# Scaling the first two tiles' queries in halves, a bank clear and a low part moved to VectorE, and a new queue order in a gated-recurrence plus two-MLP kernel

## The chip, the core and the metric

The kernel runs as one program on one core of a Trainium2 chip. The metric is device time in microseconds (us) of one execution; several executions are timed and the median is taken. Beside these, one further execution was profiled; its trace gives every row that is shown below.

## What is computed

The reference runs a gated linear recurrence over 768 steps for 4 batches of 8 heads (48 channels each), and sends its output through two MLPs. All values are 32-bit floats.

```python
for t in range(S):
    state = alpha[:, :, t, :, None] * state + k_t (outer) v_t
    y[:, :, t] = q_t . state
x = y as 3072 tokens of 384 channels
h = x @ w_in;  x = (h * cos(h)) @ w_out              # MLP 1, 2048 wide
h = max(x @ w1, x @ w2, x @ w3);  out = h @ w_out    # MLP 2, 768 wide
```

## The kernel before

**Units.** The tokens are cut into six units of 512. The recurrence of a unit is computed in tiles of heads: cumulative products of alpha (scans on VectorE, DVE in the rows) give factors with which keys and queries are scaled (GpSimd, POOL), TensorE (PE) makes scores of scaled keys with scaled queries, VectorE masks them, and PE multiplies the masked scores with the values. The first unit has its own code: three tiles of 128 rows, `chain0` (scans and scalings), `scores0` and `shared_scores0` (scores of the tile's own heads, and of the heads that are spread over the tiles), `values0` and `shared_values0` (products with the values, which add up in three PSUM banks `acc[0..2]`), `outputs0` (the sums go to SBUF as a high part, copied by ScalarE (ACT), and a low part), `transposes0` and `state0` (the state that the next unit starts from). Later units use `turn` (transposes) and `visit` (scores and states of one tile; then, as a second part, the products of a tile visited before).

**MLP 1.** It is written in steps `moe1(i)`, 96 of them, 16 per unit. A step has nine hidden matmuls (lines 763 to 765, three per group of channels `cc`; they read the unit's `xt` of that group, high and low part, and a weight's high and low part), a chain on the result, and nine output matmuls (lines 794 to 796). The chain alternates between two engines: ACT copies to whole turns (771), DVE subtracts them (772), ACT takes the sine (773), DVE multiplies (775 or 783), ACT rounds to the high part `gh` (776 or 784), DVE subtracts for the low part `gl` (777 or 789). Lines 794 and 795 of the output need `gh` alone, line 796 needs `gl`.

**Weights.** The blocks of MLP 1's weights come in by DMA while the first unit runs, and each is unpacked and split by ACT (387, 392), DVE (388, 394) and POOL (396). The weights of MLP 2 are prepared the same way later (`b_prep`, `out_prep`), and MLP 2 follows when all units are through MLP 1.

**Order.** Every operation is recorded with an engine, a planned duration, what it reads and writes, and a due time. `Program.order` plays the program through with these figures and so fixes one order per engine; each engine then works its queue strictly in that order. Constants in the head of the file (`LATE`, `ATT0`, `V2`, `MOE_EARLY`, `SLOW` and others) set due times and planned durations, so a constant can move work on all five queues. PSUM banks `ps0` to `ps4` are handed out in the same pass. Where the plan sees PE idle in the first 45 us, a filler matmul is put in (the last lines of `tile_kernel`); the kernel before has none.

Of the kernel before, what the change touches and what calls it, by code (L numbers as in the profile page):

```python
# [16 lines left out]
AF = mybir.ActivationFunctionType  # L17
# [9 lines left out]
P = 128  # L27
# [33 lines left out]
B_START, B_STEP = 17.76, 2.27  # L61
# [8 lines left out]
GLE1, GLQ = 0, 15  # L70
# [3 lines left out]
XLE = (0,)  # L74
# [4 lines left out]
GATE, GSTEP = 0, 3  # L79
LGATE = 11  # L80
W0 = -0.9
LATE, LATE_S = -3.58, -4.98
LOD = (1, 3)

W1E = 21
MOE_EARLY = 5
EARLY = 3
FIRST = -4
ATT0 = 3.97
ATTS = 3.25  # L90
VIS, VEND, VQ = 3.95, 12, 0.98
LARGE, STALL, PATIENT = 2, -0.53, 2.75
V2, V2S, TA = 16.24, 2.98, 0.97
# [168 lines left out]
def pool(n):  # L262
    return 0.16 + 0.0021 * n
# [16 lines left out]
SLOW = 1.2  # L280
# [3 lines left out]
def dma(nbytes):  # L284
    return max(nbytes, 15e3)
# [11 lines left out]
def tile_kernel(ctx, tc, aa, qk, vv, vr, wt, outT):  # L297
# [147 lines left out]
    def load0():  # L445
        def alpha(k):
            return ("inf", k), lambda: nc.sync.dma_start(al_f[k], aa[0, k, :, 0:KO]), P * KO * 4

        def keys(k, h):
            return ("inq" if h else "ink", k), lambda: nc.sync.dma_start(kq_f[k][:, HB * h:HB * (h + 1)], qk[0, k, :, HB * h:HB * (h + 1)]), P * HB * 4  # L450

        def vals(k):
            return ("v", k), lambda: nc.sync.dma_start(v_b[k], vv[0, k]), P * HB * 3

        def shared_vals():
            return "vr", lambda: nc.sync.dma_start(rest, vr.rearrange("p (i j k e) -> p i j k e", i=N2, j=2, e=32)), P * N2 * 2 * NT0 * 128

        for n, (key, f, b) in enumerate((alpha(0), keys(0, 0), alpha(1), keys(0, 1), keys(1, 0), alpha(2), keys(1, 1), keys(2, 0), keys(2, 1), vals(0), vals(1), vals(2), shared_vals())):
            op("SP", HW, f, (), [key], -40 + 0.1 * n, 0.95 * dma(b) if n else 0)

    def chain0(k):
        t, gf, kg = al_f[k], g_f[k % NGS], ("g", k % NGS)
        g = gf[:, 0:AP].rearrange("p (c t) -> p c t", c=N2)
        fv = t[:, 0:AP].rearrange("p (c t) -> p c t", c=N2)
        kv3, qv3 = views0(k)
        kf, kk, kq, ka = ("inf", k), ("ink", k), ("inq", k), ("acc", 2)
        t0 = -30 + k
        ones, seeds = acc[2][:, 0:AP // 2], acc[2][:, HB - AP // 2:][:, ::-1]
        for h in range(2):
            hs = slice(AP // 2 * h, AP // 2 * (h + 1))  # L470
            op("DVE", 0.07 + 0.00208 * AP / 2, lambda hs=hs: ve.tensor_tensor_scan(
                gf[:, 0:AP][:, ::-1][:, hs], t[:, 1:AP + 1][:, ::-1][:, hs], ones, 0.0, ALU.mult, ALU.add), [ka, kf, *([("scan", k - 1)] if k else [])], [(*kg, h)], t0)
        op("Pool", pool(HB), lambda: ge.tensor_tensor(kv3, kv3, g[:, :, 1:], ALU.mult), [(*kg, 0), (*kg, 1)], [kk], t0)
        op("Act", act(HB), lambda: se.activation(kr_b[k], kq_f[k][:, 0:HB], AF.Copy, scale=shared), [kk, "shared"], [krk[k]], t0)
        for h in range(2):
            hs, cs = slice(AP // 2 * h, AP // 2 * (h + 1)), slice(N2 // 2 * h, N2 // 2 * (h + 1))
            op("DVE", 0.15, lambda cs=cs: ve.reciprocal(seeds[:, ::CP], g[:, cs, 0]), [ka, (*kg, 1 - h)], ["seeds"], t0)
            op("DVE", 0.07 + 0.00208 * AP / 2, lambda hs=hs: ve.tensor_tensor_scan(
                t[:, hs], t[:, hs], seeds, 0.0, ALU.mult, ALU.add), [ka, "seeds", (*kg, 0), (*kg, 1)], [kf, ("scan", k)], t0)
        op("Pool", pool(HB), lambda: ge.tensor_tensor(qv3, qv3, fv[:, :, 1:], ALU.mult), [kf], [kq], t0)  # L480

    def scores0(k, n, t):
        rk, r = psum2("r0")
        kv3, qv3 = views0(k)

        def amm():
            for i in range(N2):
# [3 lines left out]
        op("PE", SLOW * 0.95, amm, [("ink", k), ("inq", k)], rk, t, tiled=True, count=32)  # L491
        return mask0(n, r, rk, t + 0.01)

    def shared_scores0(n, t):
        rk, r = psum2("r0")

        def amm(k):
            kr3, qv3 = kr_b[k].rearrange("p (c t) -> p c t", c=N2), views0(k)[1]
            for i in range(N2):
# [4 lines left out]
        for k in range(NT0):  # L504
            op("PE", SLOW * 0.95, lambda k=k: amm(k), [krk[k], ("inq", k)], rk, SR + k if k < 2 else t, tiled=True, count=32)
        return mask0(n, r, rk, t + 0.01)

    def clear0(k):
        m = zero.rearrange("p (a b) -> p a b", a=1).to_broadcast([P, 4, P])
        op("PE", 0.25, lambda: pe.matmul(acc[k].rearrange("p (a b) -> p a b", a=4), zero, m, start=True, stop=False, skip_group_check=True),  # L510
           ["zero"], [("acc", k), *(["seeds"] if k == 2 else [])], -27)
# [29 lines left out]
    def transposes0(k, t):  # L541
# [7 lines left out]
        op("PE", SLOW * N2 * 0.085, trans, [("ink", k), "ident", ("y1", LGATE)], [pk_k], t, count=2 * N2)  # L549
# [24 lines left out]
    def first_unit():  # L574
# [31 lines left out]
    def prepare(n, t0):  # L606
# [8 lines left out]
        op("SP", HW, lambda: nc.sync.dma_start(al_f[na], aa[u, p, :, 0:KO]), (), [kf], t0 - 4.8 + (0.8 if not k else 0), dma(PR * KO * 4), tiled=True)  # L615
        op("SP", HW, lambda: nc.sync.dma_start(kq_f[nk], qk[u, p]), (), [kk, kq], t0 - 3.9, dma(PR * 2 * HB * 4), tiled=True)
# [819 lines left out]
```

## Time and profile before

| what | value |
|---|---|
| median of the timed executions | 739.07 us (3 runs, 739.06 to 739.8) |
| the profiled execution, its own time | 738.83 us |
| its span, first to last instruction | 736.9 us |
| PE busy | 730.0 us, 99% of the span |
| DVE, ACT, POOL busy | 539.7 us (73%), 420.1 us (57%), 303.8 us (41%) |
| granted clock of PE | 1.00 in all 40 slices |

Times in rows count from the start of the span. What lies outside the span, 1.9 us of the profiled execution's time, belongs to start and end of the launch. A matmul's duration in a row is modelled and overlaps the next one's; what a matmul costs is read from start to start.

### The profile page before, as it was taken

The numbers are of one execution on the slowest core, as the hardware profiler recorded it, in microseconds if no ns is written. First come the engines' busy times: TensorE is split into PE (matmuls) and PEld (weight loads), VectorE is DVE, ScalarE is ACT, GpSimd is POOL, SyncE is SP. The second block draws the span as 40 slices with busy tenths as digits, with TensorE's granted clock in tenths as the row PEclk, the third lists the DMA queues.
The fourth block names the chain that finished last, engine by engine and source line by source line (L and its number), as shares of the span: only waits on it lengthen the run. The fifth ranks groups of instructions, "written<-read, shape, count | busy, mean of one in ns | idle before, by whom it ended". The sixth has DMA issues, their size and how long they took to land.

```text
span 736.9 us, 14861 instructions
## 1 busy us (share of the span) xinstructions
PE 730.0 (99%) x5815; PEld 600.8 (82%) x5815; DVE 539.7 (73%) x858; ACT 420.1 (57%) x801; POOL 303.8 (41%) x284
## 2 busy tenths in 40 slices
PE   8999999999999999999999999999999999999997
PEld 6788888888888888888888888888888888888886
DVE  7999996877877776865655666467787768677763
ACT  4888866666756666667644655443563345634233
POOL 6444433556533635454320211043465543614442
PEclk9999999999999999999999999999999999999999
DMA  8866534564644554554250111397625556246302
GB/s 319 298 226 212 171 126 134 176 222 158 206 139 154 187 181 136 184 180 148 98 207 0 44 43 44 140 368 292 213 103 201 198 177 205 77 149 206 130 1 85
DMA packets 47525, 120.41 MB, mean 163 GB/s; under 512 B 4736, under 2 KB 19968, under 8 KB 42464
## 3 DMA queue, kind: packets, MB, share of 16 engines
q1 hardware_dynamic: 47456, 119.48, 47.4%
q8 instruction: 45, 0.74, 0.4%
q14 instruction: 24, 0.20, 0.1%
HBM read 91.54 MB, written 25.95 MB: 159 GB/s over the span
## 4 chain that ended last, share of the span: by engine, by line
PE 96%; DVE 1%; ACT 1%; DMA 1%; issue 0%; SPq 0%; POOL 0%; DVEq 0%; POOLq 0%
PE acc L794 9%; PE ps L763 9%; PE acc L795 9%; PE acc L796 9%; PE ps L764 9%; PE ps L765 9%; PE ps L1147 6%; PE ps L1148 6%; PE ps L1149 6%; PE acc L1148 3%; PE acc L1147 3%; PE acc L1149 3%; PE acc L1057 2%; PE acc L1058 2%; PE acc L1056 2%; PE ps L662 2%
## 5 line engine op out<-in xcount | busy, mean ns | idle before, releaser
L763 PE MATMUL ps<-xt,wih 128*128 128x512 f32 x288 | 114.5, 397 | 0.0
L794 PE MATMUL acc<-gg,woh 128*128 128x512 f32 x288 | 114.4, 397 | 0.0
L796 PE MATMUL acc<-gg,woh 128*128 128x512 f32 x288 | 112.3, 390 | 0.2 <-DVE gg L789 0.2
L795 PE MATMUL acc<-gg,wol 128*128 128x512 f32 x288 | 112.2, 390 | 0.0
L764 PE MATMUL ps<-xt,wih 128*128 128x512 f32 x288 | 112.2, 390 | 0.0
L765 PE MATMUL ps<-xt,wil 128*128 128x512 f32 x288 | 112.2, 389 | 0.0
L772 DVE SCALAR_TENSOR_TENSOR q<-q,ps 128x512 f32<-128x512 int32 x96 | 65.5, 683 | 39.7 <-ACT q L771 39.2
L773 ACT ACTIVATE q<-q 128x512 f32<-128x512 f32 x96 | 60.4, 631 | 39.4 <-DVE q L772 39.2
L777 DVE TENSOR_TENSOR gg<-q,gg 128x512 fp32r<-128x512 f32 x81 | 62.8, 779 | 23.2 <-ACT gg L776 22.6
L771 ACT ACTIVATE q<-ps 128x512 int32<-128x512 f32 x96 | 56.9, 593 | 39.4 <-PE ps L765 37.4
L775 DVE TENSOR_TENSOR q<-q,ps 128x512 f32<-128x512 f32 x81 | 55.2, 681 | 33.0 <-ACT q L773 32.3
L776 ACT ACTIVATE gg<-q 128x512 fp32r<-128x512 f32 x81 | 51.1, 631 | 35.5 <-DVE q L775 31.1
L937 POOL TENSOR_TENSOR ar<-ar,ar 128x512 f32<-128x512 f32 x21 | 28.6, 1365 | 92.1 <-DVE as L946 67.8
L796 PEld LDWEIGHTS acc<-gg,woh 128*128 128x128 f32 x288 | 54.1, 188 | 12.1 <-DVE gg L789 0.8
L794 PEld LDWEIGHTS acc<-gg,woh 128*128 128x128 f32 x288 | 54.0, 188 | 11.8
L765 PEld LDWEIGHTS ps<-xt,wil 128*128 128x128 f32 x288 | 54.1, 188 | 11.3
L763 PEld LDWEIGHTS ps<-xt,wih 128*128 128x128 f32 x288 | 54.1, 188 | 11.1
L795 PEld LDWEIGHTS acc<-gg,wol 128*128 128x128 f32 x288 | 54.1, 188 | 10.4
L764 PEld LDWEIGHTS ps<-xt,wih 128*128 128x128 f32 x288 | 54.1, 188 | 10.4
L1155 ACT ACTIVATE q<-acc 128x512 f32<-128x512 f32 x36 | 21.5, 597 | 69.2 <-PE acc L1149 68.5
L1166 POOL TENSOR_TENSOR xf<-q 128x512 f32<-128x512 f32 x18 | 24.5, 1364 | 81.4 <-ACT q L1155 81.4
L1019 ACT ACTIVATE fs<-x 128x512 fp32r<-128x512 f32 x42 | 26.2, 630 | 44.8 <-DVE x L1170 30.0
(187 smaller groups left out, 1727.1 us busy)
## 6 DMA issues: line engine op xcount, KB each, us to landing
bs<-bfd SPq DMA_DIRECT2D x36, 1024.0 KB, 5.0
raw<-in_wt SPq DMA_DIRECT2D x56, 384.0 KB, 3.9
bfd<-bs SPq DMA_DIRECT2D x32, 384.0 KB, 2.9
kq<-in_qk SPq DMA_DIRECT2D x20, 512.0 KB, 4.4
al<-in_aa SPq DMA_DIRECT2D x23, 261.0 KB, 2.8
x1r<-yy SPq DMA_DIRECT2D x18, 256.0 KB, 2.1
ar<-x1r SPq DMA_DIRECT2D x18, 256.0 KB, 2.9
v<-in_vv SPq DMA_DIRECT2D x23, 192.0 KB, 4.5
```

Source lines behind the costliest of these rows:

```text
L763: pe.matmul(ps, wi["h"][:, f, cc], xt[:, cc, 0], start=(cc == 0), stop=False)
L764: pe.matmul(ps, wi["h"][:, f, cc], xt[:, cc, 1], start=False, stop=False)
L765: pe.matmul(ps, wi["l"][:, f, cc], xt[:, cc, 0], start=False, stop=(cc == NR - 1))
L772: op("DVE", dve(HB), lambda: ve.scalar_tensor_tensor(q, q.bitcast(I32), -TWOPI, ps, ALU.mult, ALU.add), [hk], [qk], m)
L773: op("Act", act(HB), lambda: se.activation(q, q, AF.Sin, bias=0.5 * math.pi), (), [qk], m)
L777: op("DVE", dve(HB), lambda: ve.tensor_tensor(gl, q, gh.bitcast(F32), ALU.subtract), [qk, ("gh", gn)], [("gl", gn)], m, port=True)
L794: pe.matmul(acc[c], oh, gh, start=(f == 0), stop=False)
L795: pe.matmul(acc[c], ol, gh, start=False, stop=False)
L796: pe.matmul(acc[c], oh, gl, start=False, stop=(f == NF1 - 1))
L1147: pe.matmul(bank, bt[:, i, 0], at[:, 0], start=start, stop=False, skip_group_check=skip)
L1148: pe.matmul(bank, bt[:, i, 0], at[:, 1], start=False, stop=False, skip_group_check=skip)
L1149: pe.matmul(bank, bt[:, i, 1], at[:, 0], start=False, stop=stop, skip_group_check=skip)
```

## The change

1. `HALF_Q = (0, 1)`: for tiles 0 and 1 of the first unit the scaling of the queries is two GpSimd operations of 256 columns, each waiting for its half of the scan, in place of one of 512. `score_parts` issues the matmuls of such a tile in two groups of half the chunks.
2. `zeros0` clears `acc[2]` with a memset on VectorE; before, a matmul with a zero matrix did (line 510, third of three).
3. `XLE = ()`: the low part of `xt` for group 0 is made by VectorE (the code of line 539) as for groups 1 and 2; before, a matmul with the negative identity (line 536) and an ACT copy (line 537) made it.
4. Constants: due times of visits, states, transposes, weights and MLP 2 preparation, `SLOW` (a planned duration of the first unit's matmuls) and the step from which MLP 1's chain works in place (`GLQ`, 15 to 18).

```diff
-B_START, B_STEP = 17.76, 2.27
+B_START, B_STEP = 24.54, 2.22
-GLE1, GLQ = 0, 15
+GLE1, GLQ = 0, 18
-XLE = (0,)
+XLE = ()
-LATE, LATE_S = -3.58, -4.98
+LATE, LATE_S = -3.54, -9.57
-MOE_EARLY = 5
+MOE_EARLY = 15
+HALF_K, HALF_Q = (), (0, 1)
+ZERO2 = -11.11
-ATT0 = 3.97
+ATT0 = 1.68
-SLOW = 1.2
+SLOW = 1.08
...
-        op("Pool", pool(HB), lambda: ge.tensor_tensor(qv3, qv3, fv[:, :, 1:], ALU.mult), [kf], [kq], t0)
+        if k in HALF_Q:
+            for h in range(2):
+                cs = halves0[h][1]
+                op("Pool", pool(HB // 2), lambda cs=cs: ge.tensor_tensor(qv3[:, cs], qv3[:, cs], fv[:, cs, 1:], ALU.mult), [("f0", k, h), kq], [("qp", k, h)], t0)
+        else:
+            op("Pool", pool(HB), lambda: ge.tensor_tensor(qv3, qv3, fv[:, :, 1:], ALU.mult), [kf], [kq], t0)
...
+    def score_parts(k, go, keys, rk, t):
+        parts = ((0, 1), (2, 3)) if k in HALF_Q else ((0, 1, 2, 3),)
+        for p in parts:
+            hs = sorted({i // 2 for i in p})
+            op("PE", SLOW * 0.95 * len(p) / 4, lambda p=p: go(p), [*(x for h in hs for x in (*keys(h), *queries0(k, h)))], rk, t, tiled=True, count=8 * len(p))
...
+    def zeros0(k):
+        op("DVE", 0.5, lambda: ve.memset(acc[k], 0.0), (), [("acc", k), "seeds"], ZERO2)
...
-        for k in range(NT0):
+        for k in range(NT0 - 1):
             clear0(k)
+        zeros0(NT0 - 1)
```

Over the whole program PE's queue loses two matmuls of 512 columns (lines 510 and 536) and gains one filler; the visits are as many and as much joined or split as before (25 stretches of visit matmuls in either order).

**PE, the first scores.** Before (line 489 is tile 0's own scores, line 501 the shared ones; ps1 to ps4 are PSUM banks), the last of eight rows of the one and the first of eight of the other:

```order
L489 MATMUL ps1_100<-kq0_104 128x128
L489 MATMUL ps2_101<-kq0_104 128x128
L489 MATMUL ps1_100<-kq0_104 128x128
L501 MATMUL ps3_102<-kq0_104,inv0_122 128x128
L501 MATMUL ps4_103<-kq0_104,inv0_122 128x128
L501 MATMUL ps3_102<-kq0_104,inv0_122 128x128
```

The changed kernel (521 and 533 are the same two lines, 582 is the transpose of line 547):

```order
L582 MATMUL ps0_99<-ident_78,kq0_104 128x128 x4
L521 MATMUL ps1_100<-kq0_104 128x128
L521 MATMUL ps2_101<-kq0_104 128x128
L521 MATMUL ps1_100<-kq0_104 128x128
L521 MATMUL ps2_101<-kq0_104 128x128
L533 MATMUL ps4_103<-kq0_104,inv0_122 128x128
L533 MATMUL ps3_102<-kq0_104,inv0_122 128x128
L533 MATMUL ps4_103<-kq0_104,inv0_122 128x128
L533 MATMUL ps3_102<-kq0_104,inv0_122 128x128
L521 MATMUL ps1_100<-kq0_104 128x128
```

The two kinds now alternate in groups of half the size. Between here and the first hidden matmul, the transposes of tile 2 and all four state products (`state0`) now stand in front of it; before, two of the four (line 567) stood behind the sixth hidden matmul. Tile 1's own scores go to banks ps1 and ps2, the two that tile 0's masks read; before, to ps0 and ps2.

**PE, the first output matmuls.** Before, 27 hidden matmuls (lines 763 to 765, the steps 0 to 2 of MLP 1) stand ahead of the first output; the last three of them, the transposes of the first turn (line 636) and the first outputs (acc is the bank they add up in):

```order
L763 MATMUL ps2_101<-xt0_348,wih_79 128x512
L764 MATMUL ps2_101<-xt0_348,wih_79 128x512
L765 MATMUL ps2_101<-xt0_348,wil_80 128x512
L636 MATMUL ps3_102<-ident_78,kq0_104 128x112 x4
L794 MATMUL acc0_96<-gg0_84,woh_81 128x512
L795 MATMUL acc0_96<-gg0_84,wol_82 128x512
L796 MATMUL acc0_96<-gg0_84,woh_81 128x512
```

The changed kernel has 18 hidden matmuls there (steps 0 and 1; 799 to 801 are their lines, step 0's twelfth matmul in PE's order is its last). Behind them come the same transposes (672), the filler (1389), and the first part of the first visit (698 and 702, 32 matmuls), and only then the outputs (830 to 832):

```order
L799 MATMUL ps4_103<-xt0_379,wih_79 128x512
L800 MATMUL ps4_103<-xt0_379,wih_79 128x512
L801 MATMUL ps4_103<-xt0_379,wil_80 128x512
L672 MATMUL ps1_100<-ident_78,kq0_104 128x112 x4
L1389 MATMUL ps3_102<-ident_78 128x512
L698 MATMUL ps1_100<-kq0_104 64x64
L698 MATMUL ps3_102<-kq0_104 64x64
```

Nine hidden matmuls moved from in front of the first output to behind it, and the first visit, which stood behind the outputs, to in front of it.

**ACT and DVE, the chain of steps 0 and 1.** ACT before (771, 773 and 784 are the chain, 387 and 392 weights, 750 part of a visit):

```order
L771 ACTIVATE q_83<-ps1_100 128x512
L387 ACTIVATE top1_93<-raw1_89 128x384
L750 ACTIVATE z0_113<-d0_112 48x192
L773 ACTIVATE q_83<-q_83 128x512
L392 ACTIVATE woh_81<-ps0_99 128x384
L387 ACTIVATE top0_92<-raw2_90 128x384
L784 ACTIVATE gg0_84<-ps1_100 128x512
L771 ACTIVATE q_83<-ps4_103 128x512
```

The changed kernel, ACT (807, 809 and 820 are the chain, 675 is the copy of the turn's transposes, line 639 before):

```order
L807 ACTIVATE q_83<-ps2_101 128x512
L786 ACTIVATE z0_113<-d0_112 48x192
L389 ACTIVATE top1_93<-raw1_89 128x384
L807 ACTIVATE q_83<-ps4_103 128x512
L809 ACTIVATE q_83<-q_83 128x512
L675 ACTIVATE kt0_114<-ps1_100 128x448
L809 ACTIVATE q_83<-q_83 128x512
L394 ACTIVATE woh_81<-ps0_99 128x384
L389 ACTIVATE top0_92<-raw0_88 128x384
L820 ACTIVATE gg0_84<-ps2_101 128x512
```

And its DVE (808, 819 and 825 are the chain, 390 and 396 weights, 768 a visit's mask):

```order
L808 SCALAR_TENSOR_TENSOR q_83<-q_83,ps2_101 128x512
L808 SCALAR_TENSOR_TENSOR q_83<-q_83,ps4_103 128x512
L390 SCALAR_TENSOR_TENSOR ps0_99<-raw1_89,top1_93 128x384
L819 TENSOR_TENSOR ps2_101<-q_83,ps2_101 128x512
L819 TENSOR_TENSOR ps4_103<-q_83,ps4_103 128x512
L396 TENSOR_TENSOR wol_82<-ps0_99,woh_81 128x384
L768 TENSOR_TENSOR a0_110<-ps3_102,tri_119 128x256
L825 TENSOR_TENSOR gg0_84<-ps2_101,gg0_84 128x512
```

Step 1's operations (bank ps4) now stand between those of step 0 (bank ps2): step 1's 807 ahead of step 0's 809, step 1's 808 ahead of step 0's 819. Before, step 0 went through its whole chain ahead of step 1.

## Rows read from the trace of the kernel before

**Rows 1.** The page: busy time of the engines, and the granted clock in 40 slices.

```profile
PE 730.0 (99%) x5815; PEld 600.8 (82%) x5815; DVE 539.7 (73%) x858; ACT 420.1 (57%) x801; POOL 303.8 (41%) x284
...
PEclk9999999999999999999999999999999999999999
```

**Rows 2.** Windows: from:to, length, busy (count) of PE, PEld, DVE, ACT, POOL; clock, DMA share, GB/s.

```profile
40.00:100.00 60.00, 60.00 (x688) 48.41 (x686) 56.83 (x107) 47.12 (x99) 25.87 (x29) 1.00 0.63 203
100.00:380.00 280.00, 280.00 (x3168) 231.82 (x3168) 205.60 (x353) 182.98 (x367) 127.96 (x128) 1.00 0.50 166
```

**Rows 3.** PE's timeline to the first hidden matmul: start, duration, line [idle before].

```profile
3.94 2.00 PE L1257 MATMUL ps<-ident 128*128 128x192 f32 x10
...
8.40 1.16 PE L489 MATMUL ps<-kq 48*128 48x128 f32 x16 [1.39 <-POOL kq L480]
...
12.07 1.06 PE L489 MATMUL ps<-kq 48*128 48x128 f32 x16
...
14.07 0.50 PE L510 MATMUL acc<-gg 128*128 128x512 f32 x1
14.51 0.56 PE L567 MATMUL ps<-v,bw 128*48 128x48 f32 x16
...
20.34 0.49 PE L536 MATMUL acc<-xt,gg 128*128 128x512 f32 x1
20.76 1.08 PE L517 MATMUL acc<-a,v 128*48 128x128 f32 x16
...
23.18 0.48 PE L763 MATMUL ps<-xt,wih 128*128 128x512 f32 x1
```

**Rows 4.** POOL's timeline: tile 0's query scaling.

```profile
7.17 1.17 POOL L480 TENSOR_TENSOR kq<-kq,al 128x512 f32<-128x512 f32 x1 [0.87 <-DMA kq<-in_qk]
```

**Rows 5.** DVE's timeline: tile 0's second mask, tile 1's masks.

```profile
11.50 0.68 DVE L435 TENSOR_TENSOR a<-ps,tri 128x512 f32<-128x512 f32 x1
...
13.62 1.26 DVE L435 TENSOR_TENSOR bw<-ps,tri 128x512 f32<-128x512 f32 x2
```

**Rows 6.** PE's timeline from the hidden matmuls to the first outputs and visit.

```profile
24.75 0.56 PE L567 MATMUL ps<-v,bw 128*48 128x48 f32 x16
...
25.61 0.50 PE L763 MATMUL ps<-xt,wih 128*128 128x512 f32 x1
...
26.44 0.40 PE L763 MATMUL ps<-xt,wih 128*128 128x512 f32 x1
...
30.56 0.55 PE L636 MATMUL ps<-ident,kq 112*128 112x112 f32 x4
31.03 0.50 PE L794 MATMUL acc<-gg,woh 128*128 128x512 f32 x1
...
31.93 0.50 PE L796 MATMUL acc<-gg,woh 128*128 128x512 f32 x1 [0.16 <-DVE gg L789]
...
34.80 0.39 PE L765 MATMUL ps<-xt,wil 128*128 128x512 f32 x1
...
36.29 0.50 PE L763 MATMUL ps<-xt,wih 128*128 128x512 f32 x1
```

**Rows 7.** Groups by line (page, and first 100 us): count | busy us, mean ns | idle before.

```profile
L772 DVE SCALAR_TENSOR_TENSOR q<-q,ps 128x512 f32<-128x512 int32 x96 | 65.5, 683 | 39.7 <-ACT q L771 39.2
L773 ACT ACTIVATE q<-q 128x512 f32<-128x512 f32 x96 | 60.4, 631 | 39.4 <-DVE q L772 39.2
...
L771 ACT ACTIVATE q<-ps 128x512 int32<-128x512 f32 x96 | 56.9, 593 | 39.4 <-PE ps L765 37.4
...
L639 ACT ACTIVATE kt<-ps 128x448 f32<-128x448 f32 x5 | 2.7, 545 | 0.0
```

**Rows 8.** DVE's weight steps in the first 100 us (group), and one beside POOL (timelines).

```profile
L388 DVE SCALAR_TENSOR_TENSOR raw<-raw,top 128x384 uint32<-128x384 uint32 x16 | 9.1, 569 | 0.0
...
22.48 1.19 POOL L623 TENSOR_TENSOR kq<-kq,g 112x512 f32<-112x512 f32 x1
...
22.77 1.32 DVE L388 SCALAR_TENSOR_TENSOR ps<-raw,top 128x384 uint32<-128x384 uint32 x1
```

More of the change, by code (lines that the diff above doesn't have):

```diff
@@ L468, in chain0 @@
         ones, seeds = acc[2][:, 0:AP // 2], acc[2][:, HB - AP // 2:][:, ::-1]
-        for h in range(2):
-            hs = slice(AP // 2 * h, AP // 2 * (h + 1))
+        halves0 = [(slice(AP // 2 * h, AP // 2 * (h + 1)), slice(N2 // 2 * h, N2 // 2 * (h + 1))) for h in range(2)]
+        for h, (hs, _) in enumerate(halves0):
             op("DVE", 0.07 + 0.00208 * AP / 2, lambda hs=hs: ve.tensor_tensor_scan(
-                gf[:, 0:AP][:, ::-1][:, hs], t[:, 1:AP + 1][:, ::-1][:, hs], ones, 0.0, ALU.mult, ALU.add), [ka, kf, *([("scan", k - 1)] if k else [])], [(*kg, h)], t0)
@@ L473, in chain0 @@
[L473 to L476, printed above, removed]
+                gf[:, 0:AP][:, ::-1][:, hs], t[:, 1:AP + 1][:, ::-1][:, hs], ones, 0.0, ALU.mult, ALU.add),
+               [ka, kf, *([("scan", k - 1)] if k else [])], [(*kg, h)], t0)
@@ L484, in scores0, with amm @@
         kv3, qv3 = views0(k)
-        def amm():
-            for i in range(N2):
+        def amm(p):
+            for i in p:
                 for j in range(2):
                     pe.matmul(r[j][:, i * P:(i + 1) * P], kv3[half[j], i], qv3[half[j], i], start=True, stop=True)
-        op("PE", SLOW * 0.95, amm, [("ink", k), ("inq", k)], rk, t, tiled=True, count=32)
+        score_parts(k, amm, lambda h: keys0(k, h), rk, t)
         return mask0(n, r, rk, t + 0.01)
@@ L495, in shared_scores0, with amm @@
         rk, r = psum2("r0")
-        def amm(k):
+        def amm(k, p):
             kr3, qv3 = kr_b[k].rearrange("p (c t) -> p c t", c=N2), views0(k)[1]
-            for i in range(N2):
+            for i in p:
                 for j in range(2):
@@ L504, in shared_scores0 @@
         for k in range(NT0):
-            op("PE", SLOW * 0.95, lambda k=k: amm(k), [krk[k], ("inq", k)], rk, SR + k if k < 2 else t, tiled=True, count=32)
+            score_parts(k, lambda p, k=k: amm(k, p), lambda h: [krk[k]], rk, SR + k if k < 2 else t)
         return mask0(n, r, rk, t + 0.01)
@@ L614, in prepare @@
         kf, kk, kq, vk, ik = ("inf", na), ("ink", nk), ("inq", nk), ("v", nv), ("iv", n2)
-        op("SP", HW, lambda: nc.sync.dma_start(al_f[na], aa[u, p, :, 0:KO]), (), [kf], t0 - 4.8 + (0.8 if not k else 0), dma(PR * KO * 4), tiled=True)
-        op("SP", HW, lambda: nc.sync.dma_start(kq_f[nk], qk[u, p]), (), [kk, kq], t0 - 3.9, dma(PR * 2 * HB * 4), tiled=True)
+        op("SP", HW, lambda: nc.sync.dma_start(al_f[na], aa[u, p, :, 0:KO]), (), [kf, *([*(("f0", na, h) for h in range(2))] if n < NIN else [])], t0 - 4.8 + (0.8 if not k else 0), dma(PR * KO * 4), tiled=True)
+        op("SP", HW, lambda: nc.sync.dma_start(kq_f[nk], qk[u, p]), (), [kk, kq, *([(x, nk, h) for x in ("kp", "qp") for h in range(2)] if n < NKQ else [])], t0 - 3.9, dma(PR * 2 * HB * 4), tiled=True)
         op("SP", HW, lambda: nc.sync.dma_start(v, vv[u, p]), (), [vk], t0 - 3.7, dma(P * HB * 3), tiled=True)
```

50 lines of the change are left out of this document (34 added, 16 removed).

## The prediction

> **What bounds the kernel now.** I read the page first. PE is busy for 730.0 of 736.9 us, and the clock is granted in full in every slice [rows 1]. So only what PE does, or waits for, can move the time. The windows then tell where it waits. From 40 to 100 us, and again from 100 to 380 us, PE is busy for the whole stretch [rows 2]; DVE's 57 of 60 us in the first of them shows that the next engine is close behind it there. What is open lies before 40 us, so I followed PE's timeline there. Two places stand out: PE idles 1.39 us until 8.40 for GpSimd's scaling of tile 0's queries [rows 3], and at 31.93 the first output matmul that needs `gl` is held up by DVE [rows 6]. All else up to 31 us is PE working back to back, so two matmuls fewer in PE's queue are a gain only where PE does not wait in their place.
>
> **Term 1, the halves.** GpSimd starts tile 0's queries at 7.17, when their DMA has landed, and needs 1.17 [rows 4]; PE starts 0.06 after its end [rows 3]. The trace has no scaling of 256 columns. A half costs at least half of 1.17, 0.59, and at most all of it, 1.17; I take 0.65, near the lower end, because it is the same operation with half the columns and a little fixed cost. So PE starts at 7.17 + 0.65 + 0.06 = 7.88, 0.52 earlier (0 to 0.58). The second half is done 0.65 later, while the two first groups occupy PE for about half of the 2 us that the same matmuls take undivided, so it hides.
>
> The gain doesn't last. Tile 0's second mask leaves DVE at 11.50 + 0.68 = 12.18 [rows 5]; DVE gets there by its chain of scans, which earlier scores don't shorten. Tile 1's own scores are now written to both banks that tile 0's masks read, so they start at about 12.2, against 12.07 before [rows 3]. In the time that is freed PE does tile 0's state product, work that stood later. This also holds if the halves bring nothing at all: term 1 could be 0 without moving what follows.
>
> **Term 2, the matmuls taken out.** Start to start, the clear costs 14.51 - 14.07 = 0.44 and the low part's matmul 20.76 - 20.34 = 0.42 [rows 3]. From tile 1's scores to the first hidden matmul PE needs 23.18 - 12.07 = 11.11 now [rows 3]. After the change it is 11.11 - 0.44 - 0.42, and one state product more, 0.43 (two take 25.61 - 24.75 = 0.86 [rows 6]): 10.68. I add 0.15 for the transposes, which now break up a run of tiled matmuls. The first hidden matmul then starts at 12.2 + 10.83 = 23.0, against 23.18. Tile 1's masks, done by 14.88 [rows 5], are ready: with the products, a state product and the transposes in front, PE comes for them after 15.
>
> What is gained shows nine hidden matmuls later. Before, the next one starts at 26.44, since the 0.86 of state products lies in between [rows 6]. Eighteen hidden matmuls take 30.56 - 26.44 = 4.12 [rows 6], 0.229 each, so nine end at 23.0 + 2.06 = 25.06: PE is 1.38 ahead. The memset and the low part go to DVE, 0.5 and 0.7, in front of work that PE needs only after 25; I cost them at nothing, and at up to 0.5 if `xt`'s third low part comes late.
>
> **Term 3, the first outputs.** Here it is given back. Eighteen hidden matmuls end at 23.0 + 4.12 = 27.1, not twenty-seven. Transposes: 31.03 - 30.56 = 0.47 [rows 6], to 27.6. The filler: ten 192-column matmuls take 5.64 - 3.94 us or, with the first two slow, at most their 2.00 [rows 3]; at 0.17 to 0.20 each, 512 columns in two passes cost about 0.9, to 28.5. The visit needs ACT's copy of the transposes, and ACT's queue decides that: step 1's copy to turns, which waits for the 18th matmul (27.3 with its drain), 0.59; step 0's sine, 0.63; the copy, 0.55 [rows 7]. That is 29.0 to 29.1, so the filler fills a wait. The visit's first part takes up to 36.29 - 34.80 - 0.23 = 1.26 [rows 6]; PE is through at 30.2.
>
> `gl` of step 0 comes later. Step 1's 808 follows its 807 and ends at 28.6; a weight step, 0.57 [rows 8]; step 0's multiply, 0.68 as line 772 [rows 7], to 29.8. On ACT, step 1's sine, a weight's rounding and a weight's head stand ahead of step 0's 820: three operations of 0.5 to 0.6 from 28.9 on, so it runs from about 30.5 to 31.1. DVE's `gl` ends at 31.8. PE starts the first output at 31.1, idle for 0.9, and line 796 comes at 31.85. Before it came at 31.93.
>
> At this moment PE before has done 27 hidden matmuls; now it has done 18 and a visit part. It owes 9 x 0.229 = 2.06 and has 1.26 in hand. So it is 0.8 behind; with the 0.08 that 796 is earlier, 0.7.
>
> **Term 4, afterwards.** Before, PE never idles from 40 to 380 us [rows 2]. Now the second part of the first visit stands 27 output and hidden matmuls later, with its copies on ACT behind the weights; and DVE, nearly full, decides when banks come free. I can bound this by 0 below, and above by another wait of term 3's size, 0.9. I take 0.3. Later places (`GLQ`, the due times of MLP 2's weights) move work between engines that are busy 73% or less in a stretch where PE is full, 205.60 of 280.00 for DVE [rows 2]; I cost them at nothing, and their cover is that margin.
>
> **The sum.** 0.7 + 0.3 = 1.0 slower: 738.83 of the profiled execution becomes 739.8. The median lies 0.24 above that execution, so 740.0 in the median's terms.
>
> **Rivals.** *Step 0 gets through unhindered.* Six chain operations (0.59, 0.68, 0.63, 0.68, 0.59, 0.68, the later ones taken as the earlier of their engine [rows 7]) and some 0.04 between engines make 4.1. Step 0's last matmul, the twelfth, ends at 23.0 + 12 x 0.229 + 0.17 = 25.9, so `gl` at 30.0, before the visit is through. Outputs then start at 30.2, and 796 at 30.7, 1.2 sooner: 738.8, and 738.2 if term 4 is 0 too and the visit starts earlier. It decides if step 1's matmuls end before step 0's sine could start. Against it: the queues are strict, and step 1's copy stands ahead of step 0's sine. 0.14.
>
> *DVE falls behind, slower.* A weight step took 1.32 in place of 0.57 when GpSimd scaled keys beside it [rows 8]: 0.75 each. Two such steps and a scan stand in or just ahead of the chain, and GpSimd scales the next tile's keys and queries at that time; two collisions on the path, or one and a second wait of 0.9 at the next bank, give 1.0 + 1.5 = 2.5, 741.5. It decides from the first collision after 28.6, when the path runs through DVE. For it: DVE's 95% from 40 us on [rows 2]. 0.24. The Trainium skill, "SBUF — State Buffer", section "Who interferes with whom", says that a VectorE instruction with two SBUF inputs and a GpSimd instruction that reads SBUF exclude each other for a whole instruction. By that rule every such meeting costs the loser its full wait; the 1.32 agrees with it.
>
> *The clock falls.* PE idles about 0.9 and 0.6 near 30 us. If it dropped from 2.4 to 1.2 GHz, and came back after 3 us (my assumption), 1.5 us of work would be lost: 741.5. Against it: 1.39 idle until 8.40 was followed by a full clock [rows 1, 3]. 0.02. The Trainium skill, "TensorE: Matmul & The Clock Gate", section "Part 1: The HAM clock gate", says that the gate halves the clock after idling and gives it back under load; no slice here shows a fall.
>
> **How the numbers follow.** The forecast has 0.60. A difference under 0.2%, 1.5 us, can't be told from none. The forecast lies mostly inside that; 0.06 of it passes 740.5. The unhindered chain lies inside it too, except for 0.06 below 737.6. So slower is 0.06 + 0.24 + 0.02 = 0.32, faster 0.06, same 0.62. The range reaches from 738.4, most of the unhindered case, to 741.6, where the second rival ends.
>
> **What would show it.** Right: first scores near 7.9; tile 1's scores at 12.2; the first hidden matmul near 23.0; lines 830 to 832 starting at 31 to 32 behind an idle stretch of PE that DVE or ACT ends; PE full from 40 us on but for one or two short waits. Wrong: a first hidden matmul well before 22.5 (the masks don't hold PE), first outputs before 30.5, or waits of PE after 40 us that add up to more than 1 us.

## The result, and the profile after

The changed kernel took 743.53 us (median of 6 runs, 742.85 to 744.69), the kernel before 739.54 us in the same session (6 runs, 739.06 to 740.58). The ratio is 1.0055, with a 95% interval from 1.0045 to 1.0065: 4.0 us slower, where 1.0 was forecast with a range up to 741.6. The profiled execution of the changed kernel took 742.85 us with a span of 740.9 us, 4.0 more than before.

From the page, the busy times, which answer to [rows 1], and the shares of the chain that ended last:

```profile
PE 731.7 (99%) x5815; PEld 602.1 (81%) x5815; DVE 542.1 (73%) x860; ACT 422.4 (57%) x800; POOL 307.9 (42%) x286
PE 94%; DVE 3%; ACT 1%; DMA 1%; issue 1%; POOL 0%; SPq 0%; DVEq 0%; POOLq 0%
```

PE works 1.7 us longer and waits 2.3 us more; VectorE's share of the chain has gone from 1% to 3%. The view of PE's waits (waiting line, what it waited for: us in total, times, longest; the line left out is the wait at the program's start, which both kernels have):

```profile
...
PE ps L698 <- ACT kt L675: 1.2, 1, 1.2
PE ps L521 <- POOL kq L495: 1.2, 1, 1.2
PE acc L830 <- ACT gg L820: 0.7, 1, 0.7
PE ps L799 <- DVE wol L396: 0.6, 1, 0.6
PE acc L832 <- DVE gg L813: 0.3, 1, 0.3
```

The wait for `kq` was there before (1.39). The other four are new: two between 30 and 32 us, one near 53, one near 249. PE's timeline through the first visit and the first outputs, which answers to [rows 3, 6]:

```profile
8.17 0.72 PE L521 MATMUL ps<-kq 48*128 48x128 f32 x8 [1.17 <-POOL kq L495]
...
12.43 1.16 PE L521 MATMUL ps<-kq 48*128 48x128 f32 x16
...
23.25 0.50 PE L799 MATMUL ps<-xt,wih 128*128 128x512 f32 x1
...
27.48 0.55 PE L672 MATMUL ps<-ident,kq 112*128 112x112 f32 x4
27.86 1.04 PE L1389 MATMUL ps<-ident 128*128 128x512 f32 x2
30.14 0.69 PE L698 MATMUL ps<-kq 48*64 48x64 f32 x32 [1.25 <-ACT kt L675]
...
31.92 0.80 PE L830 MATMUL acc<-gg,woh 128*128 128x512 f32 x1 [0.72 <-ACT gg L820]
32.51 0.63 PE L831 MATMUL acc<-gg,wol 128*128 128x512 f32 x1
...
33.90 0.63 PE L831 MATMUL acc<-gg,wol 128*128 128x512 f32 x1
34.33 0.63 PE L832 MATMUL acc<-gg,woh 128*128 128x512 f32 x1
...
36.30 0.39 PE L799 MATMUL ps<-xt,wih 128*128 128x512 f32 x1
```

Up to 27.9 us the forecast holds within 0.4. The visit then comes at 30.14 and not 29.05, the first output at 31.92 and not 31.1, and the outputs after it follow one another at 0.43 us in place of 0.23. The windows of the changed kernel give the reason for the last (the column behind POOL is the granted clock):

```profile
27.50:31.60 4.10, 2.45 (x71) 1.53 (x69) 2.84 (x6) 3.99 (x9) 1.98 (x4) 1.00 0.40 103
31.70:35.00 3.30, 3.08 (x7) 2.23 (x8) 3.30 (x9) 2.74 (x6) 0.95 (x1) 0.50 0.27 103
35.10:40.00 4.90, 4.90 (x81) 3.89 (x80) 3.32 (x7) 2.45 (x6) 3.26 (x4) 1.00 0.63 189
```

The clock fell from 2.4 to 1.2 GHz, from 31.68 to 35.09 us by the clock's records. The page hides this: in its 40 slices the PEclk digit is 9 everywhere. Ahead of it PE waited 1.25 us, did 64 small matmuls and waited 0.72 us; the fall came 0.24 us before this second wait ended. No single wait was as long as the 1.39 us of [rows 3], behind which the clock stayed full. All six timed executions show a mean clock of 0.997 or 0.998, about what 3.4 us at half come to. The Trainium skill, "TensorE: Matmul & The Clock Gate", "Part 1: The HAM clock gate", says that idling halves the clock and load gives it back. That agrees with the two levels here.

**A common measure.** To compare kernels whose PE orders differ, I counted the work of MLP 1 along PE's timeline, each matmul at its undisturbed cost (hidden and output 0.2285 us, a visit's 0.014 or 0.016, a transpose 0.08), and read off how much later a kernel has done the same amount than the kernel before. I call this the lag. It is good to some 0.3 us and is read from one profiled execution each. For `w_early2` the first column is read just before a wait of 1.1 us.

| kernel | lag at 37.8 us | at 52 | at 148 | at 330 | median, us | ratio, 95% interval |
|---|---|---|---|---|---|---|
| changed kernel | 2.7 | 3.8 | 3.5 | 4.1 | 743.53 | 1.0045 to 1.0065 |
| nofill | 4.2 | 5.2 | 5.1 | 5.0 | 743.15 | 1.0039 to 1.0064 |
| fill | 1.7 | 2.8 | 4.1 | 4.4 | 743.68 | 1.0046 to 1.0070 |
| fill2 | 1.5 | 2.6 | 3.7 | 5.8 | 745.90 | 1.0080 to 1.0110 |
| pad | 3.0 | 4.0 | 3.7 | 3.7 | 742.57 | 1.0036 to 1.0061 |
| z_late | 2.3 | 3.4 | 3.2 | 5.5 | 743.52 | 1.0041 to 1.0081 |
| light_act | 0.9 | 1.7 | 3.2 | 7.3 | 744.76 | 1.0061 to 1.0089 |
| w_early2 | -0.5 | 3.5 | 4.9 | 5.2 | 744.58 | 1.0061 to 1.0086 |
| w_hand | -0.1 | 6.7 | 6.4 | 6.4 | 745.55 | 1.0073 to 1.0101 |
| c_only | -0.1 | 0.7 | 3.6 | 3.9 | 742.54 | 1.0033 to 1.0060 |
| s_all | 2.3 | 2.1 | 5.6 | 6.2 | 745.19 | 1.0069 to 1.0109 |
| s_half | 0.1 | -0.1 | 5.0 | 5.4 | 744.30 | 1.0058 to 1.0083 |
| ed_half | 0.0 | 0.0 | 0.6 | 0.6 | 739.19 | 0.9995 to 1.0012 |
| ed_dve | 0.0 | 0.0 | 0.0 | 0.0 | 738.58 | 0.9988 to 1.0005 |
| ed_all | -0.2 | -0.2 | 0.0 | 0.0 | 739.01 | 0.9992 to 1.0010 |

So the changed kernel loses 2.7 us by 38 us, about 0.9 more at the bank wait near 53 us, and about 0.6 at the wait near 249.

### The profile page after: what moved, and what is told of

It is laid out like the page before. It is cut to its first block, busy times and chain, and to the rows that moved or that the text cites. A ratio compares the mean times of both kernels' runs of the same rounds, so it can differ in the third digit from the quotient of the medians.

```text
span 740.9 us, 14897 instructions
## 1 busy us (share of the span) xinstructions
PE 731.7 (99%) x5815; PEld 602.1 (81%) x5815; DVE 542.1 (73%) x860; ACT 422.4 (57%) x800; POOL 307.9 (42%) x286
## 4 chain that ended last, share of the span: by engine, by line
PE 94%; DVE 3%; ACT 1%; DMA 1%; issue 1%; POOL 0%; SPq 0%; DVEq 0%; POOLq 0%
PE acc L830 9%; PE acc L832 9%; PE acc L831 9%; PE ps L799 8%; PE ps L801 8%; PE ps L800 8%; PE ps L1183 6%; PE ps L1185 6%; PE ps L1184 6%; PE acc L1185 3%; PE acc L1183 3%; PE acc L1184 3%; PE acc L1093 2%; PE acc L1094 2%; PE acc L1092 2%; PE ps L698 2%
## 5 line engine op out<-in xcount | busy, mean ns | idle before, releaser
L811 DVE TENSOR_TENSOR q<-q,ps 128x512 f32<-128x512 f32 x78 | 53.2, 682 | 27.0 <-ACT q L809 26.3
L812 ACT ACTIVATE gg<-q 128x512 fp32r<-128x512 f32 x78 | 49.2, 630 | 34.8 <-DVE q L811 32.6
```

## The experiments

### Are the edits or the new order to blame?

The three kernels `ed_...` are the kernel before with an edit inside an operation, so that every queue keeps its order. `ed_half` has the halves:

```diff
-        op("Pool", pool(HB), lambda: ge.tensor_tensor(qv3, qv3, fv[:, :, 1:], ALU.mult), [kf], [kq], t0)
+        parts = (slice(0, N2 // 2), slice(N2 // 2, N2)) if k < 2 else (slice(0, N2),)
+        op("Pool", pool(HB), lambda: [ge.tensor_tensor(qv3[:, c], qv3[:, c], fv[:, c, 1:], ALU.mult) for c in parts], [kf], [kq], t0)
```

> The kernel before, with every queue as it was, and only the queries of tiles 0 and 1 scaled by two GpSimd instructions of 256 columns in place of one. Theory (halves are worth nothing past the masks of tile 0): the first scores begin up to 0.5 us earlier, tile 1's scores and all that follows within 0.2 us of before; 739.1, within 0.5. Rival (the two instructions cost GpSimd more than one, and the first kernel with this edit alone was slower for that): 741 or more.

`ed_dve` puts the clear and the low part on VectorE, `ed_all` does both:

```diff
-        op("PE", 0.25, lambda: pe.matmul(acc[k]...
+        op("PE", 0.25, lambda: ve.memset(acc[k], 0.0) if k == 2 else pe.matmul(acc[k]...
-            op("PE", SLOW * 0.24, lambda: pe.matmul(y, minus, ...
-            op("Act", act(HB, True), lambda: se.activation(o()[:, 1], y, AF.Copy), [yk], lk, t)
+            op("PE", SLOW * 0.24, lambda: None, ...
+            op("Act", act(HB, True), lambda: ve.tensor_tensor(o()[:, 1], y, o().bitcast(F32)[:, 0], ALU.subtract), [yk], lk, t)
```

> The kernel before, with every queue as it was, but acc[2] cleared by a memset on VectorE, and the first low part made by VectorE, each at the place in the order where TensorE's matmul stood. TensorE has two matmuls less (0.86 us), VectorE 1.2 us more. Theory (two matmuls fewer ahead of the first outputs only make TensorE wait longer there, for VectorE's low part of step 0): first hidden matmul near 22.4, a wait of 0.8 to 1.5 us at the first outputs, 739.1, within 0.7. Rival 1 (the 0.86 is gained): 738.3. Rival 2 (VectorE's 1.2 us come on the path, as it is nearly full until 100 us): 740 to 740.5.

> All three edits of the code on the kernel before, with every queue as it was (halves, memset and low part on VectorE, none of the new order). Theory (the new queue order costs the time, the edits by themselves next to nothing): 739.1, within 0.8. Rival (the edits cost it, by VectorE's 1.2 us): 740.5 or more.

All three equal the kernel before: 1.0003, 0.9997 and 1.0001. In `ed_all` the first hidden matmul starts at 22.52, 0.66 earlier than in [rows 3], and the first output that needs `gl` at 31.71, only 0.22 earlier than in [rows 6]. Two of its PE rows, and the line of its waits that shows where a part went, the masks:

```profile
22.52 0.47 PE L764 MATMUL ps<-xt,wih 128*128 128x512 f32 x1
...
31.71 0.50 PE L797 MATMUL acc<-gg,woh 128*128 128x512 f32 x1 [0.16 <-DVE gg L790]
```

```profile
PE acc L518 <- DVE bw L435: 0.4, 2, 0.3
```

So the edits by themselves neither gain nor cost anything; the 4.0 us come with the new order. The nearest to the other half of this pair is `c_only`: all constants of the changed kernel, none of the edits (`HALF_Q = ()`, `XLE = (0,)`, third clear on PE). `s_all` has the edits with the other constants of the kernel before, `s_half` the halves alone. All three were planned anew, so each has an order of its own; the exact order of the changed kernel without the edits was not run.

> All constants of the changed kernel, but none of the three edits of the code (queries in one piece, third clear and first low part on TensorE). TensorE's order then has 18 hidden matmuls, the first visit, nine hidden ones, and only then outputs. Theory (the new order costs the time, by the visit and by the third step's weights, which come later): 742 to 743.5, with a wait of 1 us or more at the first visit. Rival (the edits cost it, since they put 1.2 us on VectorE and bring TensorE to the waits earlier): 739.5 to 740.5.

> The changed kernel's three edits of the code (halves, memset on VectorE, low part on VectorE) with all other constants of the kernel before; the planner then puts 18 hidden matmuls, the transposes, three fillers, nine outputs and only then the first visit. Theory (the new queue order, above all the visit ahead of the first outputs, costs the time, the edits do not): 739.5, within 1.0. Rival (the edits themselves cost it, by bringing TensorE to the first outputs before the chain is through): 742 to 743.5, with a wait of 2 us or more, filled or not, at the first outputs.

> The kernel before with the queries' halves alone (HALF_Q), its constants and the rest unchanged; the planner keeps 27 hidden matmuls ahead of the first outputs. Theory (the 0.2 us gained at the first scores is lost at the masks, and nothing else changes): 739.4, within 0.7. Rival 1 (the halves are worth their 0.2 to 0.5 us): 739.0. Rival 2 (the halves themselves are what costs the time): 741 or more.

All three are slower, each in its own place. `c_only` took the time that was expected, but not by the wait that was expected: it has lost nothing by 38 us, and its loss comes later, 1.3 us of it in one wait (below). `s_all`, expected at 739.5, took 745.19; its lag grows from 2.2 to 5.6 between 52 and 148 us. `s_half` has no lag at 52 us and 5.0 at 148. Small waits for VectorE and ScalarE between 75 and 113 us make up half of that; the rest lies in matmuls that follow one another a little later than 0.23 us, too little to show as idle time. These are its longest waits:

```profile
...
PE acc L831 <- DVE gg L824: 1.1, 2, 0.8
PE acc L829 <- ACT gg L819: 0.7, 1, 0.7
PE acc L831 <- DVE gg L812: 0.5, 1, 0.5
PE ps L798 <- DVE yy L749: 0.4, 1, 0.4
...
```

My expectation for `s_half` failed: I took it for the halves alone, but the planner had rearranged everything behind them. `ed_half` is that experiment done rightly. With the changed kernel, four orders that were planned anew cost 3.5 to 5.8 us by the medians. The order of the kernel before, in which PE never waits from 40 to 380 us, is the exception among those measured here; that its constants were tuned until no wait was left would fit, but is not shown.

### What made PE wait near 30 us?

`z_late` is the changed kernel with one ScalarE instruction moved (304 is the operation that copies `z`, 296 the copy to `kt`):

```diff
+    order.remove(304)
+    order.insert(order.index(296) + 1, 304)
```

> The changed kernel with one instruction moved on ScalarE's queue: the copy z<-d (which waits for GpSimd) stands behind the copy of the first turn's transposes (kt) in place of four instructions ahead of it. Theory (ScalarE's wait for GpSimd puts the first visit off): the kt copy ends about 0.7 us earlier, the visit starts near 29.4 and the first outputs near 31.2; 742.8, and if the shorter waits let the clock stay full, 741.3. Rival (the weight's DMA or the sums of step 1 hold ScalarE just as long): kt within 0.2 us of where it was, 743.5.

ScalarE's timeline in the changed kernel shows what this aims at, and the one in `z_late` what it did:

```profile
27.59 0.36 ACT L786 ACTIVATE z<-d 48x192 f32<-48x192 f32 x1 [0.67 <-POOL d L776]
27.97 0.64 ACT L389 ACTIVATE top<-raw 128x384 f16<-128x384 bf16 x1
28.48 0.57 ACT L807 ACTIVATE q<-ps 128x512 int32<-128x512 f32 x1
28.95 0.62 ACT L809 ACTIVATE q<-q 128x512 f32<-128x512 f32 x1
29.46 0.54 ACT L675 ACTIVATE kt<-ps 128x448 f32<-128x448 f32 x1
```

```profile
28.48 0.53 ACT L675 ACTIVATE kt<-ps 128x448 f32<-128x448 f32 x1
```

`kt` is 0.98 earlier, the visit starts at 29.16, the outputs at 31.45. The mechanism is right, its worth small: the outputs gain 0.47, since step 0's chain on ScalarE and VectorE ends little earlier, and the clock falls all the same. The lag at 38 us is 0.4 smaller.

Why had PE nothing else to do? GpSimd's timeline shows the last step of the third hidden weight's preparation, here in the changed kernel and then in the kernel before:

```profile
34.05 1.20 POOL L398 TENSOR_TENSOR wil<-raw,wih 128x384 fp32r<-128x384 f32 x1 [2.45 <-issue]
```

```profile
27.63 1.03 POOL L396 TENSOR_TENSOR wil<-raw,wih 128x384 fp32r<-128x384 f32 x1 [0.28 <-ACT wih L392]
```

The weight is ready at 35.25 in place of 28.66, so the nine hidden matmuls of step 2 could not fill the wait. `w_early` and `w_early2` unpack it before the second output weight and put those nine matmuls behind the visit (the edit of `w_early2`, cut; operations by number; 124 to 127 unpack the hidden weight, 129 to 132 the output weight, 313 to 315 are the matmuls):

```diff
+    bank_of = lambda i: [chosen_[k] for k, v in G.of_bank.items() if i in v][0]
+    swap = {bank_of(263): bank_of(130), bank_of(130): bank_of(263)}
...
+    for a, b in ((304, 296), (124, 266), (125, 267), (296, 278), (126, 268), (127, 126), (313, 297), (314, 313), (315, 314), (285, 284), (286, 285), (129, 282), (130, 271), (131, 130), (148, 131), (132, 148)):
+        order.remove(a)
+        order.insert(order.index(b) + 1, a)
```

> The changed kernel with its queues mended by hand in one place: the third step's hidden weight is unpacked before the second output weight instead of behind it (ScalarE, VectorE, GpSimd), the copy of z stands behind the copy of kt, the nine hidden matmuls of the third step stand ahead of the first outputs instead of behind twelve of them, and two PSUM banks change places for this. Theory (TensorE waits and idles from 27.9 to 32 us since the third step's weight is ready only at 35.3, where the kernel before has it at 28.7): the weight is ready near 31, the nine hidden matmuls run between the visit and the outputs, the outputs begin near 32.8 without a wait of their own, and TensorE is 2 us or more earlier at 40 us: 741.0, or 742 to 742.5 where a wait without a releaser comes in later. Rival (VectorE is what limits this stretch, and the waits only move on to the next outputs): less than 0.7 us earlier at 40 us, 743.0 or more.

> The changed kernel with its queues mended by hand: the third step's hidden weight is unpacked before the second output weight, the copies of kt and z change places, the nine hidden matmuls of the third step stand ahead of the first outputs instead of behind twelve of them, and the second part of the first visit behind eighteen. (An earlier try at this, w_early, gave the third step's sums a PSUM bank that another sum still held, so that VectorE's product of step 0 waited for them; here the two banks change places by name.) Theory (TensorE has nothing to do from 27.9 to 32 us since the third step's weight is not ready, and the first outputs wait with it): the visit starts near 28.7, the third step's matmuls at 29.7, the outputs near 32.5 without a wait of more than 0.3; TensorE is 1.5 to 2.7 us earlier at 38 us than in the changed kernel, and the time is 741.0 to 742.0, unless the second part of the visit waits for ScalarE's copy of z. Rival (the stretch is VectorE's and ScalarE's, and what is gained at the outputs is lost at the visit's second part): 743 or more, with a wait of 1.5 us or more there.

In `w_early` two banks were exchanged by number and not by name, so that the third step's sums were added up in a bank that step 0's sum still held; VectorE waited 3.57 us there, and the run (747.05 us) says nothing on the theory. `w_early2` does: the visit starts at 28.62, step 2's matmuls at 29.60, the outputs at 32.35 without a wait, and the clock stays full to the last matmul. The lag goes from 2.7 to -0.5, so the theory holds up to there. Then it all comes back, first at the visit's second part, which waits for ScalarE's copy of `z`, as the rival had it. Its waits:

```profile
...
PE ps L723 <- ACT z L786: 1.1, 1, 1.1
PE ps L799 <- DVE wol L396: 1.0, 1, 1.0
PE ps L723 <- issue: 1.0, 1, 1.0
PE acc L830 <- ACT gg L820: 0.7, 1, 0.7
...
PE ps L801 <- POOL wil L398: 0.3, 1, 0.3
```

`w_hand` mends the next places too (masks, states and the chain of step 2 put forward):

> As w_early2, and the visit's masks and states on VectorE (two places), the second copy of z on ScalarE and the chain of step 2 are put forward, behind step 0's and step 1's low parts, so that the visit's second part and step 2's outputs find their inputs. Theory (the loss up to 38 us is one of placement, not of work): no wait over 0.5 us up to 42 us, clock full, 740.5 to 741.5. Rival (the weights of the fourth step then come later by what is put ahead of them, and TensorE waits for them instead): 742.5 or more, with waits for wil or wih near 38 us.

Here the rival is right: PE waits 2.9 us for the fourth and a later step's `wih`, 1.2 for a bank that a weight holds, 1.1 for `wil`. The lag is -0.1 at 38 us and 6.7 at 52.

```profile
PE ps L799 <- ACT wih L394: 2.9, 2, 2.4
...
PE ps L799 <- DVE wol L396: 1.2, 1, 1.2
PE ps L801 <- POOL wil L398: 1.1, 3, 0.4
```

### Is it ScalarE or VectorE that feeds PE too late?

`light_act` is the changed kernel without ScalarE's first step for each weight block (VectorE's step, behind the cut, then reads the lower part twice), `b_light_act` the same for the kernel before:

```diff
-            op("Act", act(WB) + 0.1, lambda: se.activation(upper, head, AF.Copy), [rk], [tk], due)
+            op("Act", act(WB) + 0.1, lambda: None, [rk], [tk], due)
...
```

> The changed kernel, every queue as it is, with one ScalarE instruction less in each weight block (the copy of the upper halves, 0.64 us each); VectorE's step then joins the lower part with itself, so all weights are wrong and only the times count. Theory (ScalarE's queue is what makes the third step's weight, the first visit and the first outputs late, and the later waits up to 55 us with them): the visit starts before 29.6, no wait of TensorE over 0.5 us after it, and the time is 740.5 or less. Rival (VectorE, 94% busy from 40 to 100 us, is what is late): the wait near 50 us stays, and the time is 742.5 or more.

> The same instruction left out of the kernel before (all weights wrong here too), as a control. If TensorE is what bounds the kernel before, nothing is gained: 739.0, within 0.5. Were ScalarE's queue already on the path there, 738.2 or less.

The control is 739.04 us, 0.9998 of the kernel before: ScalarE was not on the path there. In `light_act` the lag at 38 us falls to 0.9, with a full clock there; the wait for `wol` near 51 us stays, with ScalarE busy 13.12 of 20 us from 40 to 60 us and VectorE 19.74:

```profile
40.00:60.00 20.00, 19.58 (x207) 15.57 (x207) 19.74 (x39) 13.12 (x27) 9.17 (x10) 1.00 0.82 261
```

So the rival holds for the wait near 51 us, which is VectorE's. Up to 38 us ScalarE has a part: of the 1.8 us that the lag is smaller, 1.2 is the clock (below), 0.6 is left for the queue. The time itself, 744.76 us, is spoilt by what comes next.

### What does the clock's fall cost?

`nofill` leaves the filler out; `fill` and `fill2` put fillers into both waits, `fill2` with a free bank and with two warm-up matmuls fewer; `pad` has two warm-up matmuls more and is otherwise the changed kernel. The fillers of `fill2`, cut:

```diff
-                spare[i] = (m, n)
+                spare[i] = (m, n + 1)
...
+            if G.ops[i][3].__name__ == "omm" and not filled:
+                filled.append(i)
+                pe.matmul(acc[0][:, 0:3 * P]..., ident, ..., start=True, stop=True)
```

> The changed kernel without its one filler matmul; nothing else moves. Theory (the filler only fills part of a wait that ScalarE's copy ends): the first visit starts at the same 30.1 us behind a wait of about 2.2 us, the clock falls at least as early, and the time is 743.5, or up to 0.5 more where the stretch at half pace grows. Rival (the filler itself stands on the path): the visit starts up to 0.9 us earlier and the time is 742.6.

> The changed kernel with two more filler matmuls on TensorE: a second of 512 columns before the first visit, one of 384 columns before the first outputs. By the rows they fit into the two waits (1.25 and 0.72 us) and hold up nothing. Theory (the pauses let the clock fall, and the fall costs about 1.5 us): the granted clock stays full around 32 us, the output matmuls follow one another at 0.23 us, and the time is about 742.0. Rival 1 (the clock falls for another reason, such as the small matmuls of the visit): still a stretch at half the clock, 743.5. Rival 2 (the stretch at half pace costs nothing at the end, because a later wait would have taken the time anyway): full clock, but 743.2 or more.

> Again two more fillers in TensorE's two waits, but the second one writes to acc[0], which nothing uses at that time (in the first try its bank was held until VectorE had split a weight, and the outputs began 0.39 us later than in the changed kernel), and two of the seven warm-up matmuls at the program's start are left out, so that TensorE's instruction count after the outputs is that of the changed kernel. Theory (the fall of the clock costs 1.2 to 1.3 us; what took it back in the first try was the wait of 1.3 us at 126 us that no engine ends, which comes with the eight instructions more): full clock, no such wait, 742.2. Rival (the time at half pace is always taken back by later waits): 743.5.

> The changed kernel with two more warm-up matmuls of 192 columns at its start, where TensorE waits for GpSimd until 8.17 us anyway: eight instructions more, no work on the path. Theory (the wait at 126 us that no engine ends depends on where the instructions stand in the pieces in which TensorE's code is loaded): the clock falls as in the changed kernel, and a wait of 1 to 1.5 us without a releaser appears near 127 us; 744.8. Rival (that wait came by chance, or by the different times of the first try): no such wait, 743.5.

Without the filler the first visit waits 2.12 us and starts at 30.18, as expected; the clock is at half from 31.38 to 38.20, twice as long, and the lag at 38 us is 1.5 larger. Its median is none the less 743.15 (742.00 to 744.52, the profiled execution being the slowest). With the waits filled it stays full in the profiled execution, here `nofill` and then `fill2`:

```profile
31.40:38.10 6.70, 6.15 (x14) 4.62 (x15) 6.37 (x15) 4.53 (x10) 2.90 (x3) 0.50 0.55 175
```

```profile
31.70:35.00 3.30, 3.06 (x13) 2.20 (x13) 3.30 (x9) 2.57 (x5) 1.14 (x1) 1.00 0.24 93
```

The pauses are what lets the clock fall, and the fall costs 1.2 us: the lag at 38 us is 2.7 with it and 1.5 in `fill2`. The visit and the outputs start there within 0.2 of where they do in the changed kernel, so little else differs.

The mean clocks of the timed executions say the same inside one kernel, and add something. In `pad` one execution of five has a mean clock of 1.000 and took 741.94 us; the four others, with 0.997 or 0.998, took 742.37 to 743.19. In `nofill` one has 1.000 (742.00), one 0.998 (743.09), and three have 0.994 or 0.995 (743.15 to 744.52). In both, the execution without a fall is the fastest, and the same instructions in the same order let the clock fall in one execution and not in another. In `fill` four of five executions have 1.000, in `fill2` three of five 0.999 or 1.000; a mean does not tell where in the program a fall came. So the pauses make a fall likely, not certain.

Yet no time is won at the end: `fill` is 743.68, `fill2` 745.90. Waits without a releaser take it back. In `fill` there is one at 126 us, in `fill2` two, at 126 and 314 us; these are their rows in the view of waits, `fill` first:

```profile
PE ps L723 <- issue: 1.3, 1, 1.3
```

```profile
PE ps L723 <- issue: 2.7, 2, 1.8
```

`z_late` has one at 314 us (2.0), `c_only` one at 126 us (1.3), `w_early2` one at 127 us (1.0), `light_act` two (3.3 together). All stand in the middle of a visit whose two parts follow each other directly, 128 small matmuls each with its own weight load. My expectations for `pad` and `fill2` failed: `pad`, with the eight instructions more of `fill`, has none, and `fill2`, with the count of the changed kernel, has two. So the count alone does not decide.

The DMA records narrow it down. The page of the changed kernel has a queue that carries instructions (packets, MB, share):

```profile
q8 instruction: 45, 0.74, 0.4%
```

That is one packet of 16 KB for about 258 of PE's 11630 matmuls and weight loads. All eight waits stand at one of two places in PE's queue, behind 2978 to 2985 or behind 7047 to 7050 matmuls and weight loads. Each ends 1.3 to 1.6 us after the last such packet before it has landed. The other kernels, the changed one and the kernel before among them, pass the same two places without such a wait (`s_half` with one of 0.17), and there the packet had landed 2.0 us or more before PE came. So PE most likely waits for its next instructions, where small matmuls use them up faster than they arrive. What makes the packet late in some kernels and not in others is not shown.

## Why the prediction was wrong, step by step

- **Term 1** was right in kind. The first scores came at 8.17 (forecast 7.88), because the queries' DMA ended their wait only at 7.48; the two halves took 1.32 us together, 0.66 each where 0.65 was taken. Tile 1's scores came at 12.43 (12.2), and the gain was gone.
- **Term 2** was right: first hidden matmul at 23.25 (23.0), 18 in a row, transposes at 27.48 (27.1).
- **Term 3 failed by size**: 2.7 us in place of 0.7. The visit was priced at 29.05. ScalarE's copy of `z`, which waits for GpSimd until 27.59, and a weight's head stand ahead of step 1's copy. Both are in the ScalarE order shown ahead of the prediction, and its sum left both out; that made the visit 1.1 later and the first outputs 0.8 later. The other 1.2 is the clock, which the sum had put at nothing. 0.7 + 0.8 + 1.2 = 2.7, within the 0.3 of the measure.
- **The clock as a rival** had a chance of 0.02 and was priced at 1.5, from 3 us at half that were assumed. It happened, in all six executions; it lasted 3.4 us and cost 1.2. The reason against it, that 1.39 us of idling had not lowered the clock, was not enough: here two shorter waits with little work between them did. I also took the filler for a mere filling of time; without it the fall is twice as long.
- **Term 4 failed by size**: about 1.4 in place of 0.3. The bank wait near 53 us is the one that was bounded by 0.9; it cost 0.9 of lag. Later places I had costed at nothing, as VectorE has a margin there [rows 2]; the wait near 249 us cost about 0.6. It is a collision, the mechanism of the rival on VectorE, much later than I had looked for it. VectorE's scan took 2.14 us in place of the usual 1.23, beside two GpSimd scalings, and the chain's multiply (811) behind it came late (GpSimd's and VectorE's timelines):

```profile
243.90 1.20 POOL L659 TENSOR_TENSOR kq<-kq,g 112x512 f32<-112x512 f32 x1 [1.90 <-PE acc L832]
245.06 2.13 POOL L662 TENSOR_TENSOR kq<-kq,al 112x512 f32<-112x512 f32 x1
```

```profile
244.06 2.14 DVE L656 TENSOR_TENSOR_SCAN g<-al,one 112x520 f32<-112x520 f32 x1
246.12 0.66 DVE L811 TENSOR_TENSOR q<-q,ps 128x512 f32<-128x512 f32 x1
```

  The Trainium skill, "SBUF — State Buffer", "Who interferes with whom", names the port pair that VectorE and GpSimd share; the 2.14 beside 1.23 agrees with it. It is also a matter of luck: the profiled execution of `pad`, with the same order from there on, has no wait near 249 us and a lag of 3.7 at 330.
- **The range** took one rival at a time. Its upper end, 741.6, is the second rival alone; here a larger term 3, the clock and a larger term 4 came together.
- **What the method missed**: I read the new order on PE alone. That the third step's weight comes 6.6 us later stands in ScalarE's and GpSimd's queues, and it is why the planner had only a visit and a filler to offer between 27.9 and 32 us.

What stays open: why the new order delays that weight, which I did not trace to a constant, and what makes the instruction packet late before a wait without a releaser. The weight alone does not explain the end time: `w_early2` has it early and is no faster, since ScalarE and VectorE are late at the next places and an instruction wait is added. No version tried beats the kernel before by more than can be measured.

## What to carry to other kernels

When a change comes with a new order of the queues, test the edits with the order held and the order without the edits, before any price is put on an edit: here the edits give a ratio of 1.0001 and the order costs 4 us. Follow the engine that is full only to find its waits, and then ask in the queues that feed it what it could have done instead, and when that would have been ready. An idle stretch is priced by its length and by the clock behind it; short pauses can count together, and a page of 40 slices does not show the fall. Give a range room for two things going wrong at once.

## What the runs showed of the hardware

- The granted clock fell to half behind short waits: 1.25 and 0.72 us (changed kernel), 0.47 and 1.23 (`z_late`), 2.12 and 0.72 (`nofill`), each time with small matmuls between them. The stretch at half lasted 3.4 us in the first two and 6.8 in the third. By the mean clocks, one of five executions of `nofill` and one of five of `pad` had no fall.
- In `light_act` it fell in the middle of the program too, at 317.6 us for 3.4 us, behind a visit with a wait of 1.75:

```profile
313.00:317.50 4.50, 2.75 (x105) 2.35 (x97) 1.36 (x4) 1.39 (x4) 0.52 (x1) 1.00 0.32 101
317.70:320.90 3.20, 3.20 (x9) 2.43 (x8) 1.82 (x4) 1.70 (x5) 1.49 (x2) 0.50 0.66 225
```

- Waits of 1.0 to 2.0 us that no engine and none of the program's own transfers ends occur in PE's longest runs of small matmuls, in the profiles of six of these kernels and not in the kernel before. They stand at two fixed places of PE's queue and end 1.3 to 1.6 us after a 16 KB packet of instructions has landed; where the packet landed 2.0 us or more before PE came, there is no wait. That PE waits for these instructions is the likely reading; no run forced it.
